# Power-of-two scales from sums by a product with ones, an earlier third pair, and three splits on GpSimd

## The chip, the cores and the metric

The kernel runs on one core of one Trainium2 chip, as one program. The metric is the time of one execution in device microseconds; less is better. The core has five engines with instruction queues of their own: TensorE (PE, with PEld for its weight loads), VectorE (DVE), ScalarE (ACT), GpSimd (POOL), and SyncE (SP), which issues nearly all DMAs. Each queue runs in order; engines wait for each other by semaphores.

## What is computed

```python
# attention: 4 batches, 8 heads, 576 rows, 64 columns
scores = scale * np.matmul(q, k.transpose(0, 1, 3, 2))
thresh = np.max(scores, axis=-1, keepdims=True) - tau
scores = np.where(scores >= thresh, scores, -1000000000.0)
attn = softmax of scores
x = attn @ v                      # as 2304 x 512
# first layer: w_in 512 x 2048, w_out 2048 x 512
h = x @ w_in
g = P(h) / (Q(h) + 1e-06)         # a rational function of h
x = g @ w_out
# second layer, same sizes
h = x @ w_in
g = 0, (h + 1) ** 2 / 4 or h      # by h <= -1, between, h >= 1
out = g @ w_out
```

The weights come as 64-bit floats, everything else as 32-bit floats.

## The kernel before

Every fp32 operand of a large product is written as two fp16 tensors, a high part and a low part, after scaling by a power of two; a product is then three fp16 products (high by high, high by low, low by high). `split` makes the two parts. With a scale and `on_vector` it is a scaled cast on ACT (L209) and one subtraction on DVE (L210). With a scale and not `on_vector` it is a scaling in place on ACT (L212), a cast on ACT (L203) and a subtraction on GpSimd (L207).

The scale needs the largest magnitude over all 128 partitions. Each partition has one number of its own, and `everywhere` gives all partitions the maximum of them: a product with the identity turns the column into a row on every partition (PE, L182), and DVE reduces that row (L183). For the weights and for q and k of the first batch the number is a sum of squares (ACT, L241 for weights, L324 for q and k), and `root` (L163 to L167, DVE) makes the power of two and its inverse from it. For later batches it is a maximum from DVE (L328 for q and k, L296 for v), and `power` (L154 to L156) takes the place of `root`.

The PSUM tile of these products has the tag "aux" with one buffer. All tiles of that tag go through that buffer in the order in which the Python code makes them: the maxima of weight halves (`pmmw`), of q and k (`pmmqke`), of v (`pmmve`), the products `pg` of a first weight half with itself (L251, reduced by DVE in L252), the transposed row maxima (`pmr`, L556), and later the transposes of attention results (`xt`) and outputs (`pt`).

The work has these stages.

- **First attention.** Batch 0 of the attention is written in another form than the rest, in four pairs of heads: `prep_pair(0, pr)` loads q and k of a pair (tile `rqk`, one buffer), scales and splits them and transposes them by DMA (`qkT`, or `qT` and `kT` for pairs 2 and 3) with a swapped copy `kT2`; `row_max(pr)` finds the largest score of each row (PE L517/L518 into `sm` tiles, DVE L521) and puts it as three fp16 rows into `mrow` (ACT L557); then nine tiles `st{pr}` of scores (L573 to L575) are exponentiated (ACT L577), masked (DVE L578) and multiplied with v (PE L587). `row_max(pr + 1)` runs as a generator beside the nine tiles of pair pr. Beside all that, the 16 halves of the first layer's weights are made: `as_float` turns 64-bit words into fp32 (three DVE instructions, L223 to L225, per half, tile `wt`), then squares, scale, split on GpSimd, into the chunks `wc0_i`.
- **Phases.** For each batch first layer, then second layer, each in 24 steps (three blocks of 192 tokens, eight chunks of the hidden dimension). A step's first product is L834 into `ph`, its second product is L848 into `acc`, three steps later (LAG). Between them stand the activation (L719 to L728 in the first layer, L779 to L781 in the second) and a split without scale on ACT and GpSimd into `gg`. Beside the steps of the first phase the 16 halves of the second layer's weights are made (`stage_half`, tile `wh`, written to DRAM and loaded back as chunks `wc1_i`). Beside the steps of later ones stands the attention of batches 1 to 3: `attention(b)` with `prep_pair` and `prep_v`, then `att_rows` (scores `s`, DVE L419 and L381, ACT L380, split, transpose by DMA to `eT`, PE L407 into `pv`, transposes to `xT`). The first product of block 0 in phase (first layer, batch 1) needs `xT1_0`, which comes from all four pairs of batch 1.

Below, the span is cut at the first product of the first phase (218 us), at the end of that phase's work (345 us), at the first steady products of the second layer (400 us) and after the border to batch 1 (560 us). The stretch from 345 to 400 us is where the second layer's weights end, the constants of the second layer are made, and batch 1's q, k and v are prepared.

The order of instructions is not written out. Each unit of work has a priority (`at(when)`), and a scheduler with a model of its own orders each engine's queue. The first attention has 53 units:

```python
N_FIRST = 17 + 9 * NP
for n in range(N_FIRST):
    with at(36 * n / N_FIRST - 40):
        next(att)
    while halves and len(halves) * N_FIRST > 2 * NCH * (N_FIRST - 1 - n):
        with at(2.4 * (2 * NCH - len(halves)) - 40):
            i, x = halves.pop(0)
            make_half(0, i, x, chunks[0, i], False)
```

Of the kernel before, what the change touches and what calls it, by code (L numbers as in the profile page):

```python
# [10 lines left out]
F32 = mybir.dt.float32  # L11
# [28 lines left out]
def tile_attention_moe_moe2(  # L40
# [20 lines left out]
    P = 128  # L61
# [108 lines left out]
    def at(when):  # L170

        return tc.high_priority(tc.cur_priority - int(1000 * (when + 100)))

    def everywhere(name, src, n, keep=False, place=None):


        r = small(n, name, keep)
        if place is None:
            place = ps_1.tile([P, 512], F32, name="pm" + name, tag="aux")
        pm = place[:, 0 : n * P].rearrange("p (n q) -> p n q", n=n)  # L180
        for i in range(n):
            T.matmul(pm[:, i], src[:, i : i + 1].to_broadcast([P, P]), ident, start=True, stop=True)  # L182
        V.tensor_reduce(r, pm, axis=AX.X, op=ALU.max)  # L183
        return r
# [43 lines left out]
    def convert(m, i, x, dst, on_vector):  # L228
# [10 lines left out]
        hi, lo = dst[:, 0:E], dst[:, E : 2 * E]  # L239
        bound = small(1, "mb" + name)  # L240
        A.activation(hi, src, AF.Square, scale=2.0**-32, accum_out=bound)  # L241
        s = root("pw" + name, f_w[m][x][:, i : i + 1], everywhere("mw" + name, bound, 1), even=m == 1 and x == 1)
        split(hi, lo, src, s, on_vector)
        if m == 0 and x == 0:

# [66 lines left out]
    def prep_pair(b, pr, on_vector=True):  # L312
# [9 lines left out]
        if b == 0:  # L322
            for x in range(2):
                A.activation(qk[:, x, :, 0:D], raw[:, x], AF.Square, scale=2.0**-32, accum_out=mx[:, x : x + 1])  # L324
            f = small(2, f"qkf{b}_{pr}")
            s = root(f"qkr{b}_{pr}", f, everywhere(f"mqke{b}_{pr}", mx, 2), 2)
        else:
            V.tensor_reduce(mx, raw.rearrange("p x c d -> p x (c d)"), axis=AX.X, op=ALU.max, apply_absolute_value=True)  # L328
            f, s = power(f"qk{b}_{pr}", everywhere(f"mqke{b}_{pr}", mx, 2), 2)
# [127 lines left out]

    def attention(b):

        ahead = [prep_pair(b, 0)]  # L460
        yield
        vv = prep_v(b)
        yield
        xT[b] = [xp.tile([P, 2 * KT, TB], F16, name=f"xT{b}_{j}", tag="xT", bufs=NB) for j in range(NB)]
        ahead.append(prep_pair(b, 1))
        yield
        for pr in range(NP):
            pvs = {}
# [144 lines left out]
    def first_attention():  # L613
# [6 lines left out]
        for t in mrows:  # L620
            G.memset(t, 0.0)
        yield
        pairs.append(prep_pair(0, 1, False))
        yield
        for _ in row_max(0, *pairs[0][1:], mrows[0]):
            yield
        for pr in range(2, NP):
            pairs.append(prep_pair(0, pr, False))
            yield
        n = 0  # L630
        for pr in range(NP):
            data = *pairs[pr], mrows[pr % 2]
# [316 lines left out]
```

## Time and profile before

| | |
|---|---|
| time, median of 3 runs | 1276.4 us (1275.19 to 1285.7) |
| profiled execution, its own time | 1279.94 us |
| its span, first to last instruction | 1277.0 us |
| mean granted TensorE clock | 0.947 |
| busy in the span | PE 1078.5 us (84%), DVE 1021.3 us (80%), ACT 821.3 us (64%), POOL 505.1 us (40%) |

The rows come from the profiled execution, whose span is 2.9 us shorter than its own time. Times inside it count from the span's first instruction. A busy share is an average over stages with different limits, so the span is read by stages.

### The profile page before, as it was taken

What the parts mean: (1) busy time and instruction counts of PE and PEld (TensorE: products, weight loads), DVE (VectorE), ACT (ScalarE), POOL (GpSimd) and SP (SyncE); (2) the same over time, 40 slices, a digit from 0 to 9 for tenths busy, and PEclk for the clock granted to TensorE, in tenths of its full rate; (3) what the DMA queues carried; (4) which work ended last, traced back from release to release, by engine and by line L of the source; (5) the groups of instructions that cost most, each with busy time, mean ns of one, the idle gap of its engine ahead of it and who ended that gap; (6) DMA issues with size and microseconds to landing.
All of it is one profiled execution on the core that took longest, in us unless ns stands there. A gap on an engine that the chain in (4) does not pass through costs nothing.

```text
span 1277.0 us, 31136 instructions
## 1 busy us (share of the span) xinstructions
PE 1078.5 (84%) x12354; PEld 967.6 (76%) x12354; DVE 1021.3 (80%) x2403; ACT 821.3 (64%) x1477; POOL 505.1 (40%) x676
## 2 busy tenths in 40 slices
PE   2677875777755989999889999998799999999998
PEld 1344543777744878889778888998788888999997
DVE  6877869999989878679999676899998767897421
ACT  3556676776755767767676567777775666775332
POOL 3313243464434645512245455322464554222221
PEclk9787887889877999999999999999999999999999
DMA  7745445333667666871389366811793669006000
GB/s 204 228 158 167 143 165 205 126 116 120 233 222 197 101 108 130 197 182 48 73 205 224 62 121 165 224 44 37 173 239 77 107 128 251 35 2 232 34 14 26
DMA packets 220337, 176.34 MB, mean 138 GB/s; under 512 B 182048, under 2 KB 193312, under 8 KB 212000
## 3 DMA queue, kind: packets, MB, share of 16 engines
q1 hardware_dynamic: 220192, 174.36, 51.5%
q8 instruction: 96, 1.57, 0.5%
q14 instruction: 49, 0.40, 0.1%
HBM read 106.83 MB, written 21.50 MB: 100 GB/s over the span
## 4 chain that ended last, share of the span: by engine, by line
PE 38%; DVE 28%; DMA 12%; ACT 7%; issue 7%; POOL 6%; SPq 2%; DVEq 0%; ACTq 0%; POOLq 0%
PE acc L848 15%; PE ph L834 15%; DMA eT<-hl 7%; PE pv L407 2%; DVE t L727 2%; DMA qkT<-qk 2%; POOL hl L392 2%; DVE t L726 2%; DVE t L721 2%; DVE e L381 2%; DVE wt L224 2%; POOL wc L207 1%; DMA rqk<-in_k_dram 1%; DVE t L723 1%; ACT wt L212 1%
## 5 line engine op out<-in xcount | busy, mean ns | idle before, releaser
L848 PE MATMUL acc<-gg,wc 128*128 128x192 f16 x4608 | 433.3, 249 | 34.0 <-POOL gg L207 19.3
L834 PEld LDWEIGHTS <-wc 128*128 128x128 f16 x4608 | 388.5, 99 | 41.9 <-issue 24.2
L848 PEld LDWEIGHTS <-wc 128*128 128x128 f16 x4608 | 387.0, 99 | 33.5 <-issue 31.9
L207 POOL TENSOR_TENSOR gg<-t,gg 128x384 f16<-128x384 f32 x192 | 190.3, 992 | 423.1 <-ACT gg L203 348.0
L834 PE MATMUL ph<-xT,wc 128*128 128x192 f16 x2304 | 216.1, 251 | 25.6 <-ACT xT L607 10.3
L834 PE MATMUL ph<-yT,wc 128*128 128x192 f16 x2304 | 217.5, 247 | 7.3 <-DVE t L781 7.0
L392 POOL TENSOR_TENSOR hl<-e,hl 128x256 f16<-128x256 f32 x216 | 156.2, 744 | 0.0
L203 ACT CAST gg<-t 128x384 f16<-128x384 f32 x192 | 97.2, 508 | 82.3 <-DVE t L781 44.2
L381 DVE SCALAR_TENSOR_TENSOR e<-sc,nt,e 128x576 f32<-128x576 f32 x108 | 96.4, 892 | 30.8 <-ACT e L380 30.1
L780 DVE SCALAR_TENSOR_TENSOR t<-t,c 128x384 f32<-128x384 f32 x96 | 65.5, 683 | 68.8 <-ACT t L779 68.6
L390 POOL TENSOR_TENSOR hl<-e,hl 128x64 f16<-128x64 f32 x108 | 40.3, 373 | 149.2 <-ACT hl L389 145.0
L380 ACT ACTIVATE e<-sc,nt,con 128x576 f32<-128x576 f32 x108 | 93.5, 866 | 8.4 <-POOL hl L392 0.9
L389 ACT CAST hl<-e 128x576 f16<-128x576 f32 x108 | 72.2, 669 | 40.4 <-DVE e L381 39.8
L719 ACT ACTIVATE t<-ph,sc 128x384 f32<-128x384 f32 x96 | 55.3, 576 | 60.8 <-PE ph L834 60.6
L407 PE MATMUL pv<-v,eT 128*128 128x65 f16 (+3 forms) x1680 | 70.0, 194 | 26.9 <-DMA eT<-hl 26.7
L779 ACT ACTIVATE t<-ph,c 128x384 f32<-128x384 f32 x96 | 63.8, 665 | 43.2 <-PE ph L834 42.5
L419 DVE TENSOR_SCALAR_CACHE_REDUCE sc<-s 128x576 f32<-128x576 f32 x108 | 80.8, 748 | 13.0 <-PE s L374 12.7
L407 PEld LDWEIGHTS <-eT 128*128 128x128 f16 (+1 forms) x1680 | 62.4, 100 | 36.1 <-DMA eT<-hl 33.9
L207 POOL TENSOR_TENSOR wc<-wt,wc 128x256 f16<-128x256 f32 x64 | 51.6, 838 | 82.9 <-ACT wc L203 82.8
L724 ACT ACTIVATE t<-t,lc 128x384 f32<-128x384 f32 x96 | 67.8, 707 | 17.0 <-DVE t L721 16.6
L373 PE MATMUL s<-qkT 128*128 128x512 f16 (+1 forms) x240 | 63.4, 292 | 15.3 <-DVE sc L419 9.7
L726 DVE SCALAR_TENSOR_TENSOR t<-t,ka,t 128x384 f32<-128x384 f32 x96 | 64.0, 667 | 14.4 <-ACT t L725 14.2
(229 smaller groups left out, 1841.6 us busy)
## 6 DMA issues: line engine op xcount, KB each, us to landing
wc<-scratch SPq DMA_DIRECT2D x56, 1024.0 KB, 6.0
rw<-in_moe_w_in_dram SPq DMA_DIRECT2D x16, 1024.0 KB, 5.4
rw<-in_moe_w_out_dram SPq DMA_DIRECT2D x16, 1024.0 KB, 4.9
scratch<-wc SPq DMA_DIRECT2D x8, 1024.0 KB, 4.4
scratch<-wh SPq DMA_DIRECT2D x16, 512.0 KB, 3.1
rqk<-in_q_dram SPq DMA_DIRECT2D x16, 256.0 KB, 3.0
rqk<-in_k_dram SPq DMA_DIRECT2D x16, 256.0 KB, 3.0
kT<-qkT SPq DMA_DIRECT2D x28, 144.0 KB, 2.5
```

The lines of the kernel that those rows point to most:

```text
L203: A.copy(hi, src)
L207: G.tensor_tensor(lo[:, p], src[:, p], hi[:, p], op=ALU.subtract)
L380: A.activation(e, s, AF.Exp, bias=nb, scale=con[:, 0:1])
L381: V.scalar_tensor_tensor(e, s, th, e, op0=ALU.is_ge, op1=ALU.mult)
L389: A.copy(hi, e)
L392: G.tensor_tensor(lo_w[:, p], e[:, whole][:, p], hi[:, whole][:, p], op=ALU.subtract)
L407: T.matmul(pv[rows, 0:w], eT[:, c, cols], vv[:, h * NT + x if x < NT else H * NT + h, at : at + w], start=(n == 0), stop=(n == len(blocks) ...
L419: V.tensor_scalar(s, banks[:, 0:S], 1.0, -LARGEST, op0=ALU.mult, op1=ALU.max, accum_out=mx)
L724: A.activation(r, u, AF.Ln, bias=lc[:, 1:2], scale=lc[:, 0:1])
L726: V.scalar_tensor_tensor(s, s, ka[:, 0:1], r, op0=ALU.add, op1=ALU.mult)
L834: last = T.matmul(ph[:, f, :], w[:, wx, kt, f * P : (f + 1) * P], rhs, start=(n == 0), stop=(n == 3 * KT - 1))
L848: T.matmul(dst, w[:, wx, f, d * P : (d + 1) * P], gg[:, gx, f, :], start=(i == 0 and f == 0 and n == 0 and d % 2 == 0), stop=(i == NCH - 1 ...
```

## The change

It has three parts.

- `total` stands beside `everywhere`: a product of a 128 x 128 matrix of ones with the n columns gives every partition the sum over all partitions, and `root` reads it from PSUM. It has the "aux" tag too (tiles `psmw`, `psmqke`). It takes the place of `everywhere` in the four pairs of the first batch and in 24 of 32 weight halves (all but the first-matrix halves of the second layer). The scale is then made from the sum instead of the largest, so it is another power of two or the same.
- `prep_pair(0, 2)` stands ahead of `row_max(0)`, behind `prep_pair(0, 1)`. The number of units stays 53.
- In `attention(1)` pairs 0 and 1 and v are split with `on_vector` false. Pairs 2 and 3 of batch 1, and batches 2 and 3, stay as they are.

```diff
--- before.py
+++ after.py
@@ -171,6 +171,15 @@
 
         return tc.high_priority(tc.cur_priority - int(1000 * (when + 100)))
 
+    one = small(1, "one", True)
+    G.memset(one, 1.0)
+
+    def total(name, src, n):
+
+        pm = ps_1.tile([P, 512], F32, name="ps" + name, tag="aux")[:, 0:n]
+        T.matmul(pm, one.to_broadcast([P, P]), src, start=True, stop=True)
+        return pm
+
     def everywhere(name, src, n, keep=False, place=None):
 
 
@@ -239,7 +248,8 @@
         hi, lo = dst[:, 0:E], dst[:, E : 2 * E]
         bound = small(1, "mb" + name)
         A.activation(hi, src, AF.Square, scale=2.0**-32, accum_out=bound)
-        s = root("pw" + name, f_w[m][x][:, i : i + 1], everywhere("mw" + name, bound, 1), even=m == 1 and x == 1)
+        over = everywhere if m == 1 and x == 0 else total
+        s = root("pw" + name, f_w[m][x][:, i : i + 1], over("mw" + name, bound, 1), even=m == 1 and x == 1)
         split(hi, lo, src, s, on_vector)
         if m == 0 and x == 0:
 
@@ -323,7 +333,7 @@
             for x in range(2):
                 A.activation(qk[:, x, :, 0:D], raw[:, x], AF.Square, scale=2.0**-32, accum_out=mx[:, x : x + 1])
             f = small(2, f"qkf{b}_{pr}")
-            s = root(f"qkr{b}_{pr}", f, everywhere(f"mqke{b}_{pr}", mx, 2), 2)
+            s = root(f"qkr{b}_{pr}", f, total(f"mqke{b}_{pr}", mx, 2), 2)
         else:
             V.tensor_reduce(mx, raw.rearrange("p x c d -> p x (c d)"), axis=AX.X, op=ALU.max, apply_absolute_value=True)
             f, s = power(f"qk{b}_{pr}", everywhere(f"mqke{b}_{pr}", mx, 2), 2)
@@ -457,12 +467,12 @@
 
     def attention(b):
 
-        ahead = [prep_pair(b, 0)]
+        ahead = [prep_pair(b, 0, b > 1)]
         yield
-        vv = prep_v(b)
+        vv = prep_v(b, b > 1)
         yield
         xT[b] = [xp.tile([P, 2 * KT, TB], F16, name=f"xT{b}_{j}", tag="xT", bufs=NB) for j in range(NB)]
-        ahead.append(prep_pair(b, 1))
+        ahead.append(prep_pair(b, 1, b > 1))
         yield
         for pr in range(NP):
             pvs = {}
@@ -620,13 +630,13 @@
         for t in mrows:
             G.memset(t, 0.0)
         yield
-        pairs.append(prep_pair(0, 1, False))
-        yield
+        for pr in range(1, NP - 1):
+            pairs.append(prep_pair(0, pr, False))
+            yield
         for _ in row_max(0, *pairs[0][1:], mrows[0]):
             yield
-        for pr in range(2, NP):
-            pairs.append(prep_pair(0, pr, False))
-            yield
+        pairs.append(prep_pair(0, NP - 1, False))
+        yield
         n = 0
         for pr in range(NP):
             data = *pairs[pr], mrows[pr % 2]
```

In the rows of order below, names end in a running number, and the changed kernel's lines are 9 or 10 higher behind the new function (L203 is L212, L212 is L221, L241 is L250, L324 is L334, L557 is L567, L577 is L587, L779 to L781 are L789 to L791).

ACT in the first attention, from the end of pair 1's split to the first tile of pair 0, before:

```order
L203 CAST qk0_1_273<-rqk0_1_265 128x9x64 x2
L241 ACTIVATE wc0_1_146,mb0_1_1_392<-wt0_1_1_388 128x1024
L212 ACTIVATE wt0_0_1_309<-wt0_0_1_309,pw0_0_1_s_319 128x1024
L212 ACTIVATE wt0_1_0_344<-wt0_1_0_344,pw0_1_0_s_354 128x1024
L203 CAST wc0_0_145<-wt0_0_1_309 128x1024
L203 CAST wc0_1_146<-wt0_1_0_344 128x1024
L324 ACTIVATE qk0_2_506,mqk0_2_505<-rqk0_2_498 128x9x64 x2
L557 CAST mrow0_261<-pmr0_0_451 3x512
L557 CAST mrow0_261<-pmr0_4_457 3x512
L241 ACTIVATE wc0_2_147,mb0_2_0_472<-wt0_2_0_468 128x1024
L557 CAST mrow0_261<-pmr0_8_463 3x128
L577 ACTIVATE et0_0_0_585<-st0_0_0_578,con0_0_174 128x576
```

The same stretch of ACT in the changed kernel:

```order
L212 CAST qk0_1_270<-rqk0_1_262 128x9x64 x2
L334 ACTIVATE qk0_2_304,mqk0_2_303<-rqk0_2_296 128x9x64 x2
L221 ACTIVATE rqk0_2_296<-rqk0_2_296,qkr0_2_s_310 128x576 x2
L250 ACTIVATE wc0_1_148,mb0_1_1_414<-wt0_1_1_410 128x1024
...
L221 ACTIVATE wt0_0_1_334<-wt0_0_1_334,pw0_0_1_s_342 128x1024
...
L212 CAST wc0_0_147<-wt0_0_1_334 128x1024
...
L334 ACTIVATE qk0_3_528,mqk0_3_527<-rqk0_3_520 128x9x64 x2
L250 ACTIVATE wc0_2_149,mb0_2_0_474<-wt0_2_0_470 128x1024
...
L567 CAST mrow0_258<-pmr0_0_505 3x512
...
L567 CAST mrow0_258<-pmr0_4_511 3x512
L567 CAST mrow0_258<-pmr0_8_517 3x128
L587 ACTIVATE et0_0_0_565<-st0_0_0_558,con0_0_173 128x576
```

The squares and the scaling of pair 2 now stand ahead of the scaling of weight half (0, 1); the squares of pair 3 stand ahead of weight chunk 2; and `mrow0` with the first tile `et0_0_0`, which stood right behind the squares of pair 2, now stands seven rows behind the squares of pair 3.

DVE at the end of the second layer's constants (`c20_0`), before; `sc1_0_0_0` and `e1_0_0_0` are rows of batch 1's attention, `mv2` is the largest of batch 2's v, `t21_0_0_0` the activation of the second layer's first step:

```order
L767 TENSOR_TENSOR c20_0_3890<-c20_0_3890 128x8
...
L328 TENSOR_REDUCE mqk1_1_3592<-rqk1_1_3585 128x2
...
L419 TENSOR_SCALAR sc1_0_0_1_3794,mx1_0_0_1_3792<-s1_0_0_1_3787 128x576
...
L381 SCALAR_TENSOR_TENSOR e1_0_0_0_3762<-sc1_0_0_0_3758,nt1_0_0_0_3757,e1_0_0_0_3762 128x576
L780 SCALAR_TENSOR_TENSOR t21_0_0_0_3924<-t21_0_0_0_3924,c20_0_3890 128x384
L780 SCALAR_TENSOR_TENSOR t21_0_0_1_3982<-t21_0_0_1_3982,c20_0_3890 128x384
...
L183 TENSOR_REDUCE mqke1_1_3595<-pmmqke1_1_3596 128x2
L296 TENSOR_REDUCE mv2_7925<-rv2_0_7926 128x1
L781 SCALAR_TENSOR_TENSOR t21_0_0_0_3924<-ph1_0_0_0_3899,c20_0_3890,t21_0_0_0_3924 128x384
...
L781 SCALAR_TENSOR_TENSOR t21_0_0_1_3982<-ph1_0_0_1_3957,c20_0_3890,t21_0_0_1_3982 128x384
```

The same place in the changed kernel:

```order
L777 TENSOR_TENSOR c20_0_3841<-c20_0_3841 128x8
...
L790 SCALAR_TENSOR_TENSOR t21_0_0_0_3875<-t21_0_0_0_3875,c20_0_3841 128x384
L790 SCALAR_TENSOR_TENSOR t21_0_0_1_3933<-t21_0_0_1_3933,c20_0_3841 128x384
L791 SCALAR_TENSOR_TENSOR t21_0_0_0_3875<-ph1_0_0_0_3850,c20_0_3841,t21_0_0_0_3875 128x384
L791 SCALAR_TENSOR_TENSOR t21_0_0_1_3933<-ph1_0_0_1_3908,c20_0_3841,t21_0_0_1_3933 128x384
...
L338 TENSOR_REDUCE mqk1_1_3541<-rqk1_1_3534 128x2
L429 TENSOR_SCALAR sc1_0_0_0_3709,mx1_0_0_0_3707<-s1_0_0_0_3702 128x576
...
L391 SCALAR_TENSOR_TENSOR e1_0_0_0_3713<-sc1_0_0_0_3709,nt1_0_0_0_3708,e1_0_0_0_3713 128x576
L192 TENSOR_REDUCE mqke1_1_3544<-pmmqke1_1_3545 128x2
...
L306 TENSOR_REDUCE mv2_7876<-rv2_0_7877 128x1
```

The four activation rows of the second layer's first two steps now stand ahead of batch 1's attention rows and of `mv2`.

PE at the border from the second layer of batch 0 (`ph1_0_2_7` is its last first product) to the first layer of batch 1 (`ph0_1_0_0`), before; of each group of equal products one stands:

```order
L834 MATMUL ph1_0_2_7_6654<-yT0_2_4211,wc1_7_4214 128x192
...
L407 MATMUL pv1_3_1_6397<-v16_1_3438,eT1_3_1_0_6547 128x65
...
L373 MATMUL s1_3_2_1_6845<-qkT1_3_5154 128x512
...
L834 MATMUL ph1_0_2_7_6654<-yT0_2_4211,wc1_7_4214 128x192
...
L407 MATMUL pv1_3_2_6595<-v16_1_3438,eT1_3_1_1_6593 128x65
...
L373 MATMUL s1_3_2_2_6889<-qkT1_3_5154 64x512
...
L848 MATMUL acc1_0_2_6211<-gg1_0_2_3_6208,wc1_3_3683 128x192
...
L834 MATMUL ph0_1_0_0_6743<-xT1_0_3582,wc0_0_6236 128x192
...
L407 MATMUL pv1_3_2_6595<-v16_1_3438,eT1_3_1_2_6629 128x65
...
L834 MATMUL ph0_1_0_0_6743<-xT1_0_3582,wc0_0_6236 128x192
```

The same place in the changed kernel:

```order
L844 MATMUL ph1_0_2_7_6605<-yT0_2_4162,wc1_7_4165 128x192
...
L383 MATMUL s1_3_1_1_6525<-qkT1_3_5105 128x512
...
L417 MATMUL pv1_3_0_6268<-v16_1_3382,eT1_3_0_0_6266 128x65
...
L844 MATMUL ph0_1_0_0_6694<-xT1_0_3531,wc0_0_6187 128x192
...
L417 MATMUL pv1_3_0_6268<-v16_1_3382,eT1_3_0_1_6302 128x65
...
L383 MATMUL s1_3_1_2_6561<-qkT1_3_5105 128x512
...
L844 MATMUL ph0_1_0_0_6694<-xT1_0_3531,wc0_0_6187 128x192
...
L383 MATMUL s1_3_2_0_6760<-qkT1_3_5105 128x512
...
L417 MATMUL pv1_3_1_6348<-v16_1_3382,eT1_3_0_2_6346 128x65
...
L383 MATMUL s1_3_2_1_6796<-qkT1_3_5105 128x512
...
L844 MATMUL ph0_1_0_0_6694<-xT1_0_3531,wc0_0_6187 128x192
...
L383 MATMUL s1_3_2_2_6840<-qkT1_3_5105 64x512
```

The last rows of scores of batch 1's pair 3 (`s1_3_2_1`, `s1_3_2_2`) stood ahead of `ph0_1_0_0` and now stand behind its start.

## Rows read from the trace of the kernel before

**Rows 1.** Windows by stage: busy us (x instructions) of each engine, PEclk, DMA share, GB/s.

```profile
50.00:100.00 50.00, 36.59 (x182) 20.13 (x182) 37.84 (x83) 31.37 (x56) 13.44 (x15) 0.77 0.53 176
100.00:150.00 50.00, 40.86 (x234) 24.49 (x234) 38.19 (x76) 29.98 (x49) 16.96 (x22) 0.81 0.53 177
150.00:218.00 68.00, 43.38 (x243) 28.44 (x242) 56.00 (x110) 45.87 (x81) 28.04 (x34) 0.87 0.48 170
218.00:345.00 127.00, 98.75 (x1029) 93.28 (x1029) 121.06 (x215) 93.55 (x156) 60.95 (x60) 0.91 0.40 142
345.00:400.00 55.00, 27.35 (x218) 22.29 (x216) 48.60 (x145) 29.11 (x50) 19.04 (x25) 0.71 0.77 252
400.00:560.00 160.00, 142.54 (x1919) 129.59 (x1918) 125.48 (x330) 106.26 (x200) 85.21 (x133) 0.98 0.71 140
560.00:1277.00 717.00, 672.01 (x8460) 640.47 (x8457) 559.09 (x1359) 463.85 (x855) 265.95 (x358) 0.99 0.47 115
```

**Rows 2.** Groups of DVE: busy us, mean ns of one, idle before.

```profile
L210 DVE SCALAR_TENSOR_TENSOR qk<-rqk,qk_s,qk 128x576 f16<-128x576 f32 x24 | 20.5, 868 | 0.0
...
L210 DVE SCALAR_TENSOR_TENSOR v<-rv,v_s,v 128x512 f16<-128x512 f32 x15 | 12.5, 855 | 0.0
...
L183 DVE TENSOR_REDUCE mw<-pmmw 128x1 f32<-128x128 f32 x32 | 8.9, 279 | 3.4 <-PE pmmw L182 3.4
...
L183 DVE TENSOR_REDUCE mqke<-pmmqke 128x2 f32<-128x256 f32 x16 | 6.7, 416 | 3.4 <-PE pmmqke L182 3.3
```

**Rows 3.** Groups of POOL and ACT, same columns.

```profile
L207 POOL TENSOR_TENSOR wh<-wt,wh 128x256 f16<-128x256 f32 x64 | 58.6, 945 | 40.0 <-ACT wh L203 19.3 <-ACT g L757 10.6 <-issue 8.2
...
L207 POOL TENSOR_TENSOR qk<-rqk,qk 128x576 f16<-128x576 f32 x8 | 10.0, 1276 | 54.8 <-ACT qk L203 43.7 <-issue 11.1
...
L203 ACT CAST qk<-rqk 128x576 f16<-128x576 f32 x8 | 4.9, 662 | 0.0
```

**Rows 4.** Chain of waits, 45 to 112 us: start us, us, what.

```profile
60.77 2.57 POOL wc L207 x4
...
69.20 11.05 issue
...
82.91 2.91 DMA kT<-qk
```

**Rows 5.** Timeline of ACT: start us, us, engine, line, operation, idle before.

```profile
49.96 0.69 ACT L324 ACTIVATE qk<-rqk 128x576 f16<-128x576 f32 x1 [1.10 <-DMA rqk<-in_k_dram]
```

**Rows 6.** Timeline of DVE in the first attention.

```profile
58.65 0.81 DVE L578 SCALAR_TENSOR_TENSOR et<-st,con,et 128x576 f32<-128x576 f32 x1
...
78.27 0.82 DVE L578 SCALAR_TENSOR_TENSOR et<-st,con,et 128x576 f32<-128x576 f32 x1
...
112.74 0.81 DVE L578 SCALAR_TENSOR_TENSOR et<-st,con,et 128x576 f32<-128x576 f32 x1
...
145.03 0.81 DVE L578 SCALAR_TENSOR_TENSOR et<-st,con,et 128x576 f32<-128x576 f32 x1
```

**Rows 7.** Timeline of DVE at the end of the second layer's constants.

```profile
377.74 0.81 DVE L210 SCALAR_TENSOR_TENSOR qk<-rqk,qk_s,qk 128x576 f16<-128x576 f32 x1
...
381.95 0.74 DVE L210 SCALAR_TENSOR_TENSOR v<-rv,v_s,v 128x512 f16<-128x512 f32 x1
...
391.10 0.15 DVE L767 TENSOR_TENSOR c<-c 128x8 f32<-128x8 f32 x1
...
396.03 2.27 DVE L296 TENSOR_REDUCE mv<-rv 128x1 f32<-128x2048 f32 x1
398.22 0.60 DVE L781 SCALAR_TENSOR_TENSOR t<-ph,c,t 128x384 f32<-128x384 f32 x1
```

**Rows 8.** Timeline of PE where the second layer's products resume.

```profile
383.64 0.61 PE L373 MATMUL s<-qkT 128*128 128x512 f16 x1 [5.47 <-DMA qkT<-qk]
...
398.88 1.44 PE L834 MATMUL ph<-yT,wc 128*128 128x192 f16 x8 [3.96 <-DVE t L781]
```

**Rows 9.** Timeline of PE at the border to batch 1.

```profile
533.01 0.61 PE L407 MATMUL pv<-v,eT 128*128 128x65 f16 x14 [2.25 <-DMA eT<-hl]
```

## The prediction

> **What bounds the kernel now.** I read the windows by stage first [rows 1]. From 560 us on PE is busy 672.0 of 717 us, and the order there is the same before and after: I take this tail as fixed. From 218 to 345 us DVE is the bound (121.1 of 127). The rest is open: in the first attention (50 to 218 us) no engine is full, DVE has 132.0 of 168 us (37.84 + 38.19 + 56.00) and PE 120.8; from 345 to 400 us PE has 27.4 of 55 and DVE 48.6, so PE waits for a chain on DVE; from 400 to 560 us PE idles 17.5 of 160, part of it at the border to batch 1, where `pv` waits for `eT` [rows 9]. So the chain of waits and the timelines of these stages decide, not the shares of the whole span.
>
> In the first attention, the chain [rows 4] shows what is late. Pair 2's squares were done at 50.6 us [rows 5], but the chain has an unexplained wait of 11.05 us from 69.2 us, then the pair's split, its transpose to `kT` from 82.9 (2.91 us), and only then the load of pair 3, since `rqk` has one buffer. The product for pair 2's scale stands in the queue of aux tiles behind weight maxima and `mrow0`. Pair 0's masked tiles begin at 58.65 us, the last whole one of them at 78.27, and pair 1's begin at 112.74 [rows 6]. In the interlude of 34.5 us the engines wait for pair 2, then run its row maxima, and prepare pair 3.
>
> **Part 1, sums by ones.** It removes a DVE reduction per scale: 0.279 us per weight half, 0.416 per pair [rows 2]. In the first attention these are 16 halves and 4 pairs: 16 x 0.279 + 4 x 0.416 = 6.1 us of DVE work. Beside the first phase 8 more halves: 8 x 0.279 = 2.2 us. The product stays, with one or two columns in place of 128 or 256; PE has slack there, so I count nothing, and if it had none the gain would be larger. `root` now reads PSUM; no row has that read alone, so its price lies between nothing and a whole reduction of 0.279 us, which would undo the part. I take nothing: a one-column read is nearer to the other one-column rows than to a 128-column reduction. The 2.2 us lie in the DVE-bound stage and count in full: **-2.2 us**, with 0 as the other end. The 6.1 us lie in a stage that idles 36 us on DVE, so they count only together with part 2.
>
> **Part 2, pair 2 ahead.** By order, ACT has pair 2's squares and scaling right behind pair 1's split. From the squares at 50.6 I add the root, two scalings and two casts (an estimate of 5 us, the casts at 0.662 [rows 3]), two GpSimd splits of 1.276 us [rows 3] and the transpose of 2.91 us [rows 4]: `kT` of pair 2 at about 61 us instead of 85.8, and pair 3's loads start some 25 us sooner too. What this moves back: the maxima of weight half (0, 1) and all behind it pass the one aux buffer behind pair 2's; the split of a half at 60.77 [rows 4] comes at about 75. ACT then stands at pair 3's squares until its load lands, and behind them stand weight chunk 2, the product `pg` of it, and, in the aux queue behind that `pg`, `mrow0`. So pair 0's tiles begin at about 84.5 us instead of 58.65: **26 us later**. Against it stands the interlude. By order, the tiles of pair 1 follow almost at once, because the row maxima of pair 1, most of pair 2's, and the weights up to half (4, 1) now stand ahead of or among pair 0's tiles. So the stage moves by 26 less what the interlude loses. If it loses all 34.5 us the balance is -8.5. The other way of counting agrees: by order pair 2's tiles, which began at 145.03 [rows 6], begin at about the same time, with one weight half more done and the reductions behind that point gone, so pair 3, which DVE holds for most of the way (56.0 of 68 us), ends 4 to 8 us sooner. I take **-8 us** for the stage, parts 1 and 2 together. Ends: -20, if more than half of the 36 idle us is filled; +16, worked out below.
>
> **Part 3, splits on GpSimd.** DVE loses four splits of q and k and five of v: 4 x 0.868 + 5 x 0.855 = 7.7 us [rows 2]. Those of pair 0 and v, 2 x 0.81 + 5 x 0.74 = 5.3 us, lie ahead of `c20_0`, which was done at 391.2 [rows 7]. The wait that ends last for PE is L781 of the second layer's first steps, at 398.2, and PE resumes at 398.88 [rows 7, 8]. By order, these rows also pass the attention rows and `mv2` (2.27 us at 396.03), which stood between. New chain: `c20_0` at about 385.9; ACT, which has two scalings and seven casts more (0.662 us each for q and k, the same taken for v), comes to L779 at about 387.6; with L779, L780 and two L781 behind it, at some 0.65 each (L781 took 0.60, [rows 7]), PE resumes at about 390.3: **-8.5 us**. GpSimd takes 1.276 us for each of q and k [rows 3]. For v, with 512 columns, the rows give between 1.13 (1.276 by columns) and 1.89 (two of 256 columns at 0.945); I take 1.13, the nearest shape: 4 x 1.276 + 5 x 1.13 = 10.8 us. The v splits stand ahead of the first `gg` split, until about 394 us; the second product that needs it comes three steps later, which covers it; without that cover it would cost the 4 us from 390 to 394.
>
> What is given back: the attention of batch 1. Its first scores began at 383.64 us [rows 8]. The split of q and k now stands on GpSimd between the two last weight halves (4 x 0.945 us ahead of it), so the scores begin about 6 us later, while the steps begin 8.5 us sooner. By order, at the border three or four rows of scores that stood ahead of the first product of batch 1 now stand behind its start. These rows are PE work that has to be done before `xT1_0` is whole. Stalls of 2.25 us there [rows 9] already show that `pv` waits for `eT`. I give back 3.5 us, with 0 and 8.5 as the ends. Part 3: **-5 us**.
>
> A rule that speaks against part 3: GpSimd's same 128x256 subtraction took 2.57 / 4 = 0.64 us at 60.77 [rows 4] but 0.945 in the mean in the second layer's weights [rows 3], where DVE is nearly full [rows 1]. The Trainium skill, page "SBUF — State Buffer", section "Who interferes with whom", says that a DVE instruction with two SBUF inputs contends with a GpSimd instruction that reads SBUF, and that whoever comes first has the port for the whole instruction. The trace agrees in direction (0.945 against 0.64); by it DVE would wait for the added splits, the last rival below.
>
> **The sum.** -8 - 2.2 - 5 = -15.2 us. The profiled execution's 1279.94 us become 1264.7; it stands 3.5 us above the median of 1276.4, so the forecast for the median is 1261.2, say **1262 us**. One per cent is 12.8 us, about what a measurement of this kernel can tell from no change.
>
> **Rivals.**
> *The border takes it back (1271 us).* For: attention of batch 1 lags by order, and PE already waits for `eT` [rows 9]. The full 8.5 us return, the first attention gains only 3: -3 - 2.2 - 0 = -5. Against: the waits seen there are short, and the rows behind the border do not all wait.
> *Slower: the aux buffer (1290 us).* Place: ACT at pair 3's squares and `mrow0` behind `pg` of chunk 2. Pair 0's tiles start 26 us later, and if the interlude is only thinned, because the weights displaced into pair 0's tiles stretch these, little comes back. Price: 26 less what the interlude loses; the whole change turns slower when that is under 19 us (26 - 19 = +7 against -7.2 from the other stages), with 10 us it is +16, and with nothing left from part 3, +16 - 2.2 = +14. For: 30 us of DVE time have to be repacked, and DVE has only 36 idle in the stage. Against: order shows no block of row maxima between the two pairs any more.
> *More (1246 us).* The first attention gains 20 us, as the whole stage packs denser, and the border gives nothing back: -20 - 2.2 - 8.5 = -30.7.
> *GpSimd's splits hold up DVE (1269 us).* If each of the nine splits (10.8 us) stops DVE's two-input instructions for its length, DVE loses more than the 7.7 us it is relieved of: part 3 is +3, the sum -8 - 2.2 + 3 = -7. For: 0.945 against 0.64. Against: ACT ends that chain by then, not DVE. The page named above would make this the rule.
>
> **How the numbers follow.** Forecast, -10 to -20 us: 0.45. Border: 0.23. Slower: 0.15. More: 0.11. GpSimd: 0.06. Four fifths of the forecast's chance lie beyond 12.8 us: faster 0.36 + 0.11 = 0.47. Slower: nine tenths of its rival, 0.135. Same: the rest, 0.395. The range leaves out the slower rival and half of "more": 1247 to 1283 us.
>
> **What would show it.** In the changed profile: pair 2's split on GpSimd near 56 us, not 80; pair 0's first masked tile near 84; pair 1's near 115; the first first-layer product near 209, not 217; no L210 for q, k and v near 380; L779 near 388 and PE resuming 8 us after that stage's shift; more idle at the border before batch 1's first layer. I am wrong if pair 1's tiles start past 125 us, if ACT waits longer than 10 us for pair 3, or if PE between 518 and 560 us idles 8 us more than before.

## The result, and the profile after

The changed kernel takes 1285.9 us in the median of 20 runs, the kernel before 1278.5 us in 20: a ratio of 1.0059, interval 1.0043 to 1.0075, or 7.5 us slower. That is outside the range of the forecast and on its other side. The profiled execution took 1282.74 us, with a span of 1281.0, 4.0 us more than the span before. The profiled pair shows about half of the difference of the medians, since that of the changed kernel is one of its faster executions (1281.37 to 1295.52), and that of the kernel before (1279.94) lies above its median.

The windows, cut at the changed kernel's own stages (columns as in [rows 1]):

```profile
50.00:100.00 50.00, 37.44 (x194) 20.61 (x194) 37.43 (x80) 32.13 (x48) 24.20 (x28) 0.67 0.67 209
100.00:150.00 50.00, 42.63 (x252) 26.95 (x250) 42.98 (x84) 36.45 (x65) 12.30 (x16) 0.93 0.46 160
150.00:212.00 62.00, 42.51 (x228) 28.08 (x228) 48.73 (x100) 43.93 (x76) 23.02 (x30) 0.84 0.47 170
212.00:349.00 137.00, 104.72 (x1085) 99.85 (x1084) 125.30 (x218) 95.87 (x159) 62.25 (x61) 0.90 0.42 146
349.00:392.00 43.00, 16.29 (x134) 13.99 (x133) 34.23 (x112) 26.16 (x46) 21.43 (x27) 0.66 0.68 223
392.00:560.00 168.00, 148.97 (x1954) 134.37 (x1954) 131.96 (x337) 111.29 (x210) 92.87 (x136) 0.98 0.71 150
560.00:1281.00 721.00, 670.50 (x8449) 637.89 (x8445) 559.87 (x1363) 463.25 (x855) 265.84 (x360) 0.99 0.47 114
```

DVE's busy time in the first three windows is 129.1 us (37.43 + 42.98 + 48.73) where it was 132.0, and the first attention, which ended at 220 us, now ends at 212. The last window is what the prediction took as fixed: PE is busy 1.5 us less than in [rows 1] (670.5 for 672.0), and the stretch is 4 us longer.

The timeline of DVE in the first attention, the rows that answer to [rows 6], the first tiles of pairs 0, 1 and 2:

```profile
81.76 1.53 DVE L588 SCALAR_TENSOR_TENSOR et<-st,con,et 128x576 f32<-128x576 f32 x2
...
113.09 1.54 DVE L588 SCALAR_TENSOR_TENSOR et<-st,con,et 128x576 f32<-128x576 f32 x2 [0.74 <-ACT et L587]
...
142.19 1.54 DVE L588 SCALAR_TENSOR_TENSOR et<-st,con,et 128x576 f32<-128x576 f32 x2 [0.28 <-ACT et L587]
```

The timeline of POOL, pair 2's split:

```profile
54.10 2.51 POOL L216 TENSOR_TENSOR qk<-rqk,qk 128x576 f16<-128x576 f32 x2 [15.10 <-ACT qk L212]
```

Pair 2 is split at 54.1 us (80.3 before), and pair 0's tiles begin at 81.8, 23 us later than in [rows 6]; pair 1's begin at the old time and pair 2's 3 us earlier. Up to here the trace is the predicted one. The timeline of DVE at the constants of the second layer, which answers to [rows 7]:

```profile
382.71 0.86 DVE L755 TENSOR_TENSOR w2b<-f_w,sr 128x8 f32<-128x8 f32 x1
383.50 1.16 DVE L772 TENSOR_SCALAR c<-sr,rk_s 128x8 f32<-128x8 f32 x1
384.57 1.16 DVE L773 TENSOR_SCALAR c<-sr,rk_s 128x8 f32<-128x8 f32 x1
385.64 1.17 DVE L772 TENSOR_SCALAR c<-sr,rk_s 128x8 f32<-128x8 f32 x1
386.72 0.22 DVE L774 TENSOR_SCALAR c<-sri,rk_f 128x8 f32<-128x8 f32 x1
...
388.26 0.15 DVE L777 TENSOR_TENSOR c<-c 128x8 f32<-128x8 f32 x1
...
391.53 1.13 DVE L791 SCALAR_TENSOR_TENSOR t<-ph,c,t 128x384 f32<-128x384 f32 x2
```

What POOL does then, and when PE resumes ([rows 8]):

```profile
379.51 2.56 POOL L216 TENSOR_TENSOR wh<-wt,wh 128x256 f16<-128x256 f32 x4
...
382.43 4.35 POOL L216 TENSOR_TENSOR v<-rv,v 128x512 f16<-128x512 f32 x4
390.07 1.12 POOL L216 TENSOR_TENSOR v<-rv,v 128x512 f16<-128x512 f32 x1 [3.30 <-ACT v L212]
```

```profile
392.19 3.68 PE L844 MATMUL ph<-yT,wc 128*128 128x192 f16 x22 [6.42 <-DVE t L791]
```

ACT's L789 waits there for the last row of the constants, `c` of L777:

```profile
388.26 1.23 ACT L789 ACTIVATE t<-ph,c 128x384 f32<-128x384 f32 x2 [5.19 <-DVE c L777]
```

Three instructions on 8 columns take 1.16 us each while GpSimd has splits of v (4.35 us for four, from 382.43); the same form takes 0.22 once they are over. In the kernel before, where DVE has these splits, the first of them is

```profile
388.34 0.22 DVE L762 TENSOR_SCALAR c<-sr,rk_s 128x8 f32<-128x8 f32 x1
```

The marks of several kernels side by side, each from the trace of one profiled execution (us): the end of the last L608 row of the first attention (changed kernel L618), the second layer's first product, the first second-layer product after the constants (PE resumes), the first product of the second layer in batch 1, and the end of the span.

| kernel | first attention ends | second layer begins | PE resumes | second layer, batch 1 | end |
|---|---|---|---|---|---|
| before | 220.0 | 353.1 | 398.9 | 668.4 | 1277.0 |
| changed | 212.1 | 348.7 | 392.2 | 666.7 | 1281.0 |
| sums alone (e1) | 213.1 | 346.3 | 390.8 | 663.5 | 1283.5 |
| third pair alone (e2) | 226.2 | 355.1 | 397.4 | 663.3 | 1274.0 |
| GpSimd alone (e3) | 218.9 | 351.4 | 392.6 | 664.4 | 1280.0 |
| changed, ones in place (e9) | 212.2 | 349.0 | 392.1 | 662.9 | 1275.5 |
| sums and third pair in place (e10) | 218.5 | 355.3 | 394.0 | 671.1 | 1283.6 |
| sums in place (e11) | 209.9 | 342.9 | 386.4 | 652.1 | 1267.4 |
| sums in place again (e15) | 210.8 | 343.8 | 389.3 | 661.4 | 1277.2 |

The changed kernel leads by 7.9 us at 212, by 4.4 where the second layer begins, by 6.7 at PE's resumption and by 1.7 at the next mark, and ends 4.0 behind. So the first phase is the first stretch that went another way: 136.6 us for 133.1. One execution of a kernel differs from the next by some us in each of these columns (e11 and e15 are the same program); the ratios below, not this table, say what a kernel is worth.

### The profile page after: what moved, and what is told of

Same layout as the page of the kernel before. It is cut to its first block, busy times and chain, and to the rows that moved or that the text cites. A ratio compares the mean times of both kernels' runs of the same rounds, so it can differ in the third digit from the quotient of the medians.

```text
span 1281.0 us, 31116 instructions
## 1 busy us (share of the span) xinstructions
PE 1079.1 (84%) x12346; PEld 968.6 (76%) x12346; DVE 1014.0 (79%) x2366; ACT 825.9 (64%) x1486; POOL 515.2 (40%) x686
## 4 chain that ended last, share of the span: by engine, by line
PE 34%; DVE 14%; DMA 11%; issue 5%; POOL 4%; ACT 3%; SPq 2%; DVEq 0%; ACTq 0%; POOLq 0%
PE acc L858 15%; PE ph L844 14%; DMA eT<-hl 6%; POOL hl L402 3%; PE pv L417 2%; DMA qkT<-qk 2%; DVE e L391 1%; DMA rqk<-in_k_dram 1%; DVE sc L429 1%; POOL gg L216 1%; DVE t L736 1%; DVE t L737 1%; DVE t L790 1%; PE s L383 1%; DVE t L738 1%
## 5 line engine op out<-in xcount | busy, mean ns | idle before, releaser
L844 PE MATMUL ph<-xT,wc 128*128 128x192 f16 x2304 | 218.3, 252 | 17.4 <-DVE t L733 11.8
L844 PE MATMUL ph<-yT,wc 128*128 128x192 f16 x2304 | 220.5, 249 | 7.5 <-DVE t L791 7.1
L212 ACT CAST gg<-t 128x384 f16<-128x384 f32 x192 | 97.2, 508 | 79.1 <-DVE t L791 40.9
L789 ACT ACTIVATE t<-ph,c 128x384 f32<-128x384 f32 x96 | 63.8, 666 | 50.3 <-PE ph L844 44.8
L736 DVE SCALAR_TENSOR_TENSOR t<-t,ka,t 128x384 f32<-128x384 f32 x96 | 67.5, 703 | 10.2 <-ACT t L735 9.8
```

Of the source, the lines that this page charges most:

```text
L212: A.copy(hi, src)
L736: V.scalar_tensor_tensor(s, s, ka[:, 0:1], r, op0=ALU.add, op1=ALU.mult)
L844: last = T.matmul(ph[:, f, :], w[:, wx, kt, f * P : (f + 1) * P], rhs, start=(n == 0), stop=(n == 3 * KT - 1))
```

## Experiments

The theory after the result: **GpSimd**, the splits of batch 1 on GpSimd cost more than the other parts gain. Its rivals: **first attention**, the earlier third pair costs time, and **sums**, the new scale costs time by itself. When the first four runs had spoken for "sums", this was split again: **addresses**, the new tile of ones takes 32 bytes of SBUF and moves all later tiles, against sums by order, PSUM read or scales. All ratios are to runs of the kernel before on the same chip.

| run | kernel | ratio (95%) |
|---|---|---|
| e1 | sums alone | 1.0037 (1.0017 to 1.0057) |
| e2 | third pair alone | 0.9988 (0.9968 to 1.0008) |
| e3 | GpSimd alone | 1.0002 (0.9979 to 1.0025) |
| e4 | sums and third pair | 1.0047 (1.0024 to 1.0070) |
| e5 | before, spare tile of 4 bytes | 1.0042 (1.0020 to 1.0065) |
| e6 | changed, shift of 64 bytes | 1.0045 (1.0022 to 1.0068) |
| e7 | sums, shift of 64 | 1.0060 (1.0035 to 1.0085) |
| e8 | sums and third pair, shift of 64 | 1.0043 (1.0022 to 1.0065) |
| e9 | changed, in place | 1.0016 (0.9991 to 1.0041) |
| e10 | sums and third pair, in place | 0.9998 (0.9978 to 1.0018) |
| e11 | sums, in place | 0.9943 (0.9921 to 0.9966) |
| e12 | before, spare tile of 128 bytes | 1.0066 (1.0043 to 1.0089) |
| e13 | before, shift from qkT on | 0.9991 (0.9963 to 1.0019) |
| e14 | before, shift from qk on | 1.0059 (1.0033 to 1.0084) |
| e15 | e11 again | 0.9968 (0.9944 to 0.9992) |
| e16 | sums and GpSimd, in place | 1.0025 (1.0003 to 1.0047) |
| e17 | changed in place, v on DVE | 1.0023 (0.9999 to 1.0048) |
| e18 | e16 with v on DVE | 0.9998 (0.9978 to 1.0017) |

### The parts alone (e1 to e4)

Each run takes parts of the change's diff and leaves the others out; the scheduler orders each kernel anew.

> Part 1 alone (sums by ones); order of pairs and splits of batch 1 as before. Theory GpSimd (the splits of batch 1 on GpSimd cost what the other parts gain): 0 to -5 us against the kernel before. Theory first attention (the earlier third pair costs time there): 0 to -3 us. Rival sums (the read of PSUM by root or the new order of the weights costs time): +3 to +8 us.

> Part 2 alone (pair 2 ahead of the row maxima of pair 0). Theory GpSimd: -2 to -6 us, with the first attention ending some 4 us sooner. Theory first attention: +4 to +8 us. Rival sums: -2 to -6 us.

> Part 3 alone (splits of batch 1's v and pairs 0 and 1 on GpSimd). Theory GpSimd: +5 to +12 us, with small DVE instructions of about 1.1 us each under the splits of v, and the loss spread from the constants of the second layer to the border of batch 1. Theory first attention and rival sums: 0 to -5 us.

> Parts 1 and 2 without part 3. Theory GpSimd: -4 to -9 us against the kernel before, so 11 to 16 us below the changed kernel. Theory first attention: +4 to +8 us. Rival sums: +2 to +6 us.

The sums alone cost 5 us, the two other parts nothing that can be told from zero. That is the rival "sums", against both other theories (e4 by itself would also fit "first attention", which e2 rules out). But the first attention of e1 ends 7 us earlier than before, as sums were meant to do; the loss comes behind 660 us, where no instruction of the new function is left and e1's order is that of the kernel before.

### A tile that nobody uses (e5 to e8)

```diff
# e5, the kernel before
+    small(1, "spare", True)
     def at(when):
# e6, e7, e8: the changed kernel, sums alone, sums and third pair
-    one = small(1, "one", True)
+    one = small(9, "one", True)[:, 0:1]
```

A tile of this pool takes 32 bytes or a multiple of it, so e5 moves all later tiles by 32 bytes, as the change does, and e6 to e8 by 64.

> The kernel before with one unused 4-byte tile where the new function has its ones: every later SBUF tile lies 32 bytes further, no instruction and no order changes. Theory addresses (the sums' loss comes from the 32-byte shift, which moves the tiles that DMAs read and write): +4 to +8 us, most of it after 660 us. Rival sums (order, PSUM read or the other scales): 0, within 1.5 us.

> The changed kernel with the ones in a tile of 36 bytes, which takes 64, so later tiles lie 64 bytes further than before; the order is that of the changed kernel. Theory addresses: -1 to -6 us against the kernel before. Rival sums: +5 to +8 us, as the changed kernel.

> Part 1 alone with the 64-byte shift; order as in sums alone. Theory addresses: 0 to -4 us. Rival sums: +3 to +6 us, as sums alone.

> Parts 1 and 2 with the 64-byte shift; order as in the run with both. Theory addresses: -2 to -8 us. Rival sums: +4 to +8 us.

e5 alone settles that the shift costs time: the same instructions in the same order, and 1.0042. Of the theories only "addresses" allows that. Its guess that 64 bytes would be a good shift failed: e6 to e8 stand at 1.0043 to 1.0060, where it asked for a gain or none of the loss. The view by tile of `qkT` shows what is slower, the transposes from `qk`, which SP's queue issues (min, median and max in ns); the kernel before, and then e5:

```profile
L340 SPq DMA_TRANSPOSE qkT<-qk x14: 1752/1906/4902, 18.2 to 991.5; - x14
```

```profile
L340 SPq DMA_TRANSPOSE qkT<-qk x14: 2436/2746/4627, 18.7 to 995.1; - x14
```

1.91 us in the median become 2.75. The changed kernel:

```profile
L350 SPq DMA_TRANSPOSE qkT<-qk x14: 2549/2736/4634, 18.1 to 994.2; - x14
```

### No shift (e9 to e11), and a shift of 128 bytes (e12)

```diff
-    ln_e = small(1, "ln_e", True)
+    two = small(2, "ln_e", True)
+    ln_e, one = two[:, 0:1], two[:, 1:2]
     G.memset(ln_e, LN_E)
...
-    one = small(1, "one", True)
     G.memset(one, 1.0)
# e12, the kernel before
+    small(32, "spare", True)
```

> The changed kernel with the ones in the unused second column of a tile that both kernels have (ln_e), so that all large tiles lie where the kernel before has them; order as in the changed kernel. Theory addresses (now: any shift that breaks the old offsets, 32 or 64 bytes alike, slows the transposes qkT from qk, 2.33 to 3.06 us at issue in the spare-tile run): transposes back near 2.3 us, and -1 to -6 us against the kernel before. Rival sums (order, PSUM read, other scales): +5 to +8 us, as the changed kernel.

> Parts 1 and 2 with the ones in the same unused column, no tile shifted. Theory addresses: -2 to -8 us against the kernel before. Rival sums: +4 to +6 us.

> Part 1 alone, no tile shifted. Theory addresses: 0 to -4 us against the kernel before. Rival sums: +3 to +6 us, as sums alone.

> The kernel before with an unused tile of 128 bytes in place of 4: all later tiles 128 bytes further. Theory addresses: 0, within 2 us, with transposes near 2.3 us, if a multiple of 128 bytes is enough; +4 to +7 us with transposes near 3.0 us if it takes 256. Rival (any other layout costs, whatever the transposes take): +4 to +7 us with transposes near 2.3 us.

With the ones in an unused column the transposes of the changed kernel are back:

```profile
L350 SPq DMA_TRANSPOSE qkT<-qk x14: 1791/2018/6269, 17.4 to 989.2; - x14
```

and its ratio goes from 1.0059 to 1.0016: the shift cost about 5.5 us of its 7.5. In the waits of PE from 400 to 668 us, the row of `pv` for `eT` (us in total, times, longest) is, in the kernel before, in the changed kernel and then with the ones in place:

```profile
PE pv L407 <- DMA eT<-hl: 13.9, 13, 2.9
```

```profile
PE pv L417 <- DMA eT<-hl: 20.1, 13, 3.2
```

```profile
PE pv L417 <- DMA eT<-hl: 15.9, 10, 3.4
```

The lead at the second layer of batch 1 is 5.5 us in this execution and not 1.7. In e9 the theory held in its transposes, not in its range (it asked for -1 to -6 us; +2 was measured, not to be told from zero). e10 misses its range too (-2 to -8 us; none was measured), and e11 passes its own (0 to -4) on the good side: sums alone, in place, gain 7 us, the best kernel of the study. e12's 128 bytes cost as much as 32, with 2.71 us in the median for the transposes; so where `qk` lay before was a good place, and not each multiple of 128 bytes from it is one. 256 bytes weren't tried.

### Which tile (e13, e14)

```diff
# e13: qk is 32 bytes wider, so it stays and all behind it moves
-        qk = ap.tile([P, 2, C, 2 * D], F16, ...)
+        qk = ap.tile([P, 2 * C * 2 * D + 16], F16, ...)[:, 0 : 2 * C * 2 * D].rearrange(...)
# e14: an unused tile ahead of qk
+    ap.tile([P, 1], F32, name="spare", tag="spare", bufs=1)
```

> The kernel before with the tile of qk 32 bytes wider: qk, the inputs and the weights stay where they were, qkT and all later tiles lie 32 bytes further; order as before. Theory transposes (the transposes' longer issue and landing are the loss): +3 to +6 us if they stand near 3.0 us at issue, within 1.5 us of the kernel before if they stand near 2.3 (then the source address counts). Rival later tiles (the loss comes from tiles behind qkT): +3 to +6 us whatever the transposes take.

> The kernel before with an unused 32-byte tile ahead of qk: qk and all later tiles lie 32 bytes further, weight chunks and input tiles stay; order as before. Theory transposes: transposes near 3.0 us and +3 to +6 us. Rival inputs (the loss comes from weight chunks or loaded tiles that move): within 1.5 us.

e13's transposes, then e14's:

```profile
L340 SPq DMA_TRANSPOSE qkT<-qk x14: 1749/1950/4481, 18.2 to 990.5; - x14
```

```profile
L340 SPq DMA_TRANSPOSE qkT<-qk x14: 2454/2732/5227, 18.3 to 997.7; - x14
```

With `qk` in its place nothing is lost, though every tile behind it moves; with `qk` moved too the transposes take 2.73 us and the kernel 1.0059. Chunks and input tiles stay where they were in both, so they are out. It is the address of `qk`, the source of the transposes. 14 of them at 0.73 us more in the mean (2.33 in the kernel before, 3.06 in e5) are 10 us of SP's queue, which has all other DMAs of the attention behind them; how these become 5 to 8 us at the end was not followed transfer by transfer.

### The parts in place (e15, e16), and v on DVE (e17, e18)

```diff
# e17, e18
-        vv = prep_v(b, b > 1)
+        vv = prep_v(b)
```

> The same kernel as sums in place, again. Theory third pair (in place, the sums gain 6 us and the third pair loses that): -4 to -8 us against the kernel before. Rival chance (the earlier run was a lucky one): -3 to 0 us.

> Parts 1 and 3 without part 2, ones in the unused column, no tile shifted. Theory third pair: -5 to -10 us against the kernel before, at least as good as sums alone in place. Rival (GpSimd's splits cost what they free, whatever part 2 does): -5 to 0 us and 1 to 4 us above sums alone in place.

> The changed kernel with the ones in place and the splits of v of batch 1 on DVE again; those of q and k of pairs 0 and 1 stay on GpSimd. Theory port (DVE's small instructions wait for GpSimd's splits of v): small DVE instructions back at 0.22 us, 37 to 39 us from the phase's first product to PE's resumption (43.1 with v on GpSimd), and 1275 to 1280 us. Rival order (the scheduler's other order costs it, not the port): 42 us or more there, with small instructions at 0.22.

> Part 1 in place with q and k of batch 1's pairs 0 and 1 split on GpSimd, v on DVE, third pair as before. Theory port: 41 to 45 us there (47.2 with v on GpSimd), and -3 to -8 us against the kernel before. Rival order: 46 us or more, and 0 to +4 us.

e15 gives 0.9968: the gain of the sums is there again, 4 us by this run and 7 by e11. On top of it the third pair brings the ratio to 0.9998 (e10), GpSimd to 1.0025 (e16), both to 1.0016 (e9). In medians on the same chip e10 is 6.0 us above e11, e9 8.0 above e11, and e16 7.2 above e15 (against e15's ratio, from another chip, e10 is 4 us above): both parts that cost nothing alone cost 4 to 8 us on top of the sums. e16 fits neither of its ranges: it is 3 us above the kernel before, where the theory of the third pair asked for -5 to -10 and its rival for -5 to 0. So the third pair is not the only part that takes the gain back.

For GpSimd one place is seen. From the second layer's first product to PE's resumption, kernels with parts 1 and 2 take 38.1 to 38.8 us (e4, e8, e10), with part 3 added 43.1 to 43.7 (e9, e6, the changed kernel). In the 12 us ahead of the first L789 there, DVE's small instructions (39 to 42) keep it busy for 6.6 us in e10, 8.8 in e17 with q and k on GpSimd, and 11.8 in e9 with v too; DVE's own splits there take 4.7, 3.7 and 0. The sums are 11.3, 12.5 and 11.8: what DVE gave away came back as longer small instructions. The same four rows in e10, in the timeline of DVE, without GpSimd's splits of q, k and v (the first of them still under a split of a weight half):

```profile
386.27 0.71 DVE L772 TENSOR_SCALAR c<-sr,rk_s 128x8 f32<-128x8 f32 x1
386.89 0.22 DVE L773 TENSOR_SCALAR c<-sr,rk_s 128x8 f32<-128x8 f32 x1
387.02 0.22 DVE L772 TENSOR_SCALAR c<-sr,rk_s 128x8 f32<-128x8 f32 x1
387.16 0.22 DVE L774 TENSOR_SCALAR c<-sri,rk_f 128x8 f32<-128x8 f32 x1
```

Instructions of this form take 1.16 us in the five kernels with v's splits on GpSimd (the changed one, e3, e6, e9, e16) and at most 0.96 in the fifteen others, of which the kernel before is one: at 680.3 us it has one of 0.96, beside a split of `gg`. But the slow rows don't set the price by themselves. In e3 this stretch takes 41.2 us, 4.6 less than in the kernel before, with these rows in it:

```profile
383.68 1.16 DVE L763 TENSOR_SCALAR c<-sr,rk_s 128x8 f32<-128x8 f32 x1
```

In e17 they are 0.23 us, but the products of two tiles for batch 1's first layer (L692 to L696), which stand ahead of them in that order, fall under the splits of q, k and the weights. In its timeline of DVE:

```profile
382.38 1.00 DVE L692 TENSOR_TENSOR mb<-hb,binv 128x1 f32<-128x1 f32 x1
383.42 1.20 DVE L693 TENSOR_TENSOR mb<-hb,mb 128x1 f32<-128x1 f32 x1
384.65 0.59 DVE L694 TENSOR_TENSOR mb<-mb,binv 128x1 f32<-128x1 f32 x1
385.28 0.59 DVE L695 TENSOR_TENSOR mb<-hb,mb 128x1 f32<-128x1 f32 x1
...
387.53 0.23 DVE L772 TENSOR_SCALAR c<-sr,rk_s 128x8 f32<-128x8 f32 x1
```

and of POOL:

```profile
382.08 2.52 POOL L216 TENSOR_TENSOR qk<-rqk,qk 128x576 f16<-128x576 f32 x2
384.56 2.54 POOL L216 TENSOR_TENSOR wh<-wt,wh 128x256 f16<-128x256 f32 x4
```

So e17 resumes after 41.9 us: below 43.1, but not at the 37 to 39 that the theory named, and at the edge of what its rival did. e18 (44.8 against 47.2 for e16) lies inside the theory's 41 to 45, but its time doesn't: 0.9998, where the theory asked for -3 to -8 us and the rival for 0 to +4. The port theory holds for the small instructions; that the order carries the rest is not shown, and how much of each can't be told from these runs. The times of e3, e16, e17 and e18 carry something more: there the scheduler's order is also another one from 905 to 1002 us, while the changed kernel and e9 have the order of the kernel before.

For the third pair, on top of the sums the first attention ends at 212.0 to 218.5 us in seven profiles (mean 215.0) and without it at 209.9 to 213.1 in six (mean 211.4). That is 3.6 us. The first phase behind it takes 136.6 to 138.2 us in these seven and 132.9 to 134.3 in the six, another 3.7 in the mean; why was not found. Without part 3 the stretch to PE's resumption then gives some 6 us back (38.1 to 38.8 for the 43.5 to 46.2 of sums alone). Alone, the third pair ends the first attention 6 us later than before (e2).

## Why the prediction was wrong, step by step

By the profiled pair, -15.2 us were forecast and +4.0 measured. Of the 19.2 between them the first attention has none, the first phase 5.7 (+3.5 for -2.2), the constants 6.2 (-2.3 for -8.5), the border 1.5 (+5.0 for +3.5) and the tail 5.7 (for 0). By the ratios the shift of addresses accounts for some 5.5 us of the loss, and what the parts take back from each other is in the rest. None of the three signs came by which the prediction was to be known wrong: pair 1's tiles started at 113 us, ACT waited 5.5 us for pair 3, and PE idled 6.6 us from 518 to 560 where it had idled 6.0.

- **First attention, -8 us.** The size was right (220.0 to 212.1), and the marks on the way too (54, 82 and 113 us for 56, 84 and 115; pair 2's tiles at 142, for about the 145 of before). The credit was not: the sums alone give 7 to 10 us there, and the third pair takes some back. The step that failed is "so they count only together with part 2": the 6.1 us of reductions count without it. That they lay on a path that waited, and that more was gained than their own time because PE and ACT waited for them, was not measured by itself.
- **Beside the first phase, -2.2 us.** The step that failed is "count in full". With the sums alone in place the phase takes 133.0 us (e11, e15), as before (133.1), so nothing of the 2.2 us is seen; with the third pair on top it takes 136.6 to 138.2. The sum took no loss of part 2 behind the first attention into account, and what loses there is open.
- **At the constants, -8.5 us.** From the second layer's first product to PE's resumption the time went from 45.8 to 43.5 us. The step that failed is "`c20_0` at about 385.9". It is counted on the times of before; with the 10.2 us forecast for the stages ahead it stands for 375.7, and `c20_0` came at 388.4. From e10 to e9 GpSimd took 4.7 us of splits off DVE in the 12 us ahead of L789, and its small instructions took 5.2 us more. This is the last rival's mechanism, with the place wrong: it was weighed for DVE's large instructions, and "ACT ends that chain by then" spoke against it; ACT waited 5.2 us for `c20_0` instead. The page "SBUF — State Buffer" of the Trainium skill, section "Who interferes with whom", names `tensor_scalar` among the DVE instructions that can contend with GpSimd, and says that whoever issues first has the shared ports for the whole instruction. The trace agrees with it: 1.16 us beside splits of 1.12, and 0.22 without.
- **The border, 3.5 us given back.** Of the lead of 6.7 us, 5.0 were gone at the second layer of batch 1; with the ones in place 1.3 of 6.8. Two executions of one program differ by more than that in this stretch (265.7 us in e11, 272.1 in e15), so the size of the term is neither borne out nor refuted, and the share of the shift in it is not shown.
- **"I take this tail as fixed."** It failed. The order there is the same, but from the second layer of batch 1 to the end the stretch went from 608.7 to 614.3 us. Its windows in the kernel before, the changed kernel, e9 and e15 (columns as in [rows 1]):

```profile
668.36:1277.00 608.64, 574.87 (x7327) 548.54 (x7326) 456.28 (x1120) 383.48 (x712) 236.27 (x322) 1.00 0.48 116
```

```profile
666.70:1281.00 614.30, 575.76 (x7327) 548.30 (x7326) 457.09 (x1120) 383.77 (x712) 235.34 (x322) 0.99 0.47 116
```

```profile
662.93:1275.50 612.57, 579.74 (x7327) 552.73 (x7326) 457.03 (x1120) 384.16 (x712) 235.38 (x322) 0.99 0.47 116
```

```profile
661.42:1277.20 615.78, 581.50 (x7327) 554.63 (x7326) 457.69 (x1120) 384.05 (x712) 234.47 (x322) 0.98 0.48 115
```

In the profiled pair nearly all of it is waiting: PE idles 38.5 us where it idled 33.8, and is busy 0.9 us longer. With the ones in place the idle time is back (32.8 in e9, 34.3 in e15), and another loss shows: the same 7327 products take PE 4.9 and 6.6 us longer than in the kernel before. The granted clock is lower there, 0.987 and 0.984 in the mean for 0.996 (0.994 in the changed kernel), that is, for some us more at the lower of its two levels, 1.2 and 2.4 GHz. Where it fell, PE had just waited, mostly 1.6 to 3.0 us for `eT` or `sc`; the kernel before waits at several of the same places and keeps its clock, so why it falls is open. Nothing in the rows of before could show that a constant of 4 bytes would be the dearest part of the change.
- **The aux buffer**, the rival with the other sign, gave the right sign by a mechanism that didn't occur in the size it named: pair 0's tiles started 23 us later, but the interlude shrank from 34.5 us to 6 (106.85, the last tile of pair 0, to 113.09), as the forecast had it.

## What to carry to other kernels

A new constant can move every tile behind it, and the same instructions in the same order can then take another time; before a small edit is judged, run the kernel with the tile alone and the edit without the shift. Work that is moved to GpSimd can cost DVE something even where DVE no longer does it: here 0.22 us became 1.16 in small instructions of a chain. Parts that cost nothing alone can take away each other's gain, so take them one by one in the layout in which they will stay: here the sums alone, with the ones in an unused column, beat the kernel before by 0.3 to 0.6%.

## What the runs showed that was not expected

- A transpose by DMA from `qk` to `qkT` took 1.91 to 2.14 us at issue (medians of eleven profiles) with `qk` in its old place, and 2.71 to 2.75 (nine) with it 32, 64 or 128 bytes further. Not each transpose is slower at issue: those from `qk` to `qT` and `kT`, two each, took 1.29 and 1.39 us before and 1.30 and 1.33 in e14 (though 2.9 and 3.4 to 3.5 to landing), and `eT` from `hl`, which moved as well, kept 1.5 us in the mean.
- A DVE instruction on 8 columns took 0.22 us alone and 1.16 us beside GpSimd splits of 1.12 us each.
- The last stretch, from the second layer of batch 1 on, in the kernels that have the order of the kernel before there: without the sums 608.7 to 610.7 us with `qk` in its place (three profiles) and 611.9 to 614.2 with it moved (three); with the sums 612.5 to 615.8 (four) and 614.3 to 621.6 (six). The idle time of PE follows the shift, 31 to 35 us in the seven in place and 33 to 41 in the nine moved. What the sums add in place is mostly PE's busy time at a lower granted clock (0.984 to 0.989 for 0.989 to 0.996), in one execution of each; whether the other scales in the data, the small tiles that lie elsewhere, or chance does it stays open.
